# Two-stage DFT and mixture of experts on one core: the pass over the expert weights starts with the first batch, through four buffers

## The chip, the cores and the metric

One Trainium2 chip, one of its cores. The metric is device microseconds of the whole program, from the run's own time; a profile of one execution shows what each engine did. TensorE (PE) multiplies matrices, VectorE (DVE), ScalarE (ACT) and GpSimd (POOL) work on vectors, and SyncE (SP) issues most of the DMAs. Each engine works through its own list of instructions in order and waits at the head of that list.

## The reference, cut to what matters

```python
# x: 8 batches x 2496 rows x 256 columns
X = np.fft.fft(np.fft.fft(x, axis=1), axis=2).real
x = X.reshape(19968, 256)
e_idx = np.argmax(x @ w_gate, axis=1)            # one of 8 experts for each row
gate_w = softmax(x @ w_gate)[e_idx];  eom = sigmoid(x @ w_output_gate)
for e in range(8):
    mask = e_idx == e
    h = np.maximum(x[mask] @ w1[e], 0.0)         # w1[e]: 256 x 1024
    out[mask] = gate_w * eom * (h @ w2[e])       # w2[e]: 1024 x 256
```

## The kernel before

**Front end.** Each batch of `x` comes in five chunks `xt` of 512 KB. A chunk is folded in two parts: `fold1` (three instructions, most of them on POOL) and `fold2` (mostly DVE, result `ft`). The first DFT stage (`dstage`, matrices `tdet` and `tdot`) multiplies the five folded chunks, `devac` writes the result as a high and a low half in f16 (`ahi` on ACT, `alo` on DVE), and the second stage (`sstage`, tables `tst`, `tstm`, `tstr`, `tstq`) runs in five steps a batch. `sevac` turns a step's result into rows of the transform, `gating` picks the expert of each row, and 20 indirect DMAs a batch (`scatter`, tile `scr`), issued by POOL, write the rows into a scratch tensor sorted by expert. `steps` counts the steps over all batches: step n is step n % 5 of batch n // 5. Before a batch can be multiplied, its energy must be known: ACT squares the folded chunks (`sq`), DVE adds (`es`), PE sums over partitions, and `scale` makes a power of two from it.

**Weight energies.** The expert weights are split into f16 halves with a power of two for each expert and each matrix. For it every weight (16 tiles of 128x2048 f32, 1 MB each, `wt`) is loaded once, squared and summed on ACT (`wsquare`), and `wscales` makes the scales from the sums. The tiles have two buffers (`NW`); load k + 2 is issued by SP after square k.

**Expert stage.** The loop breaks out after step FSTART = 13, and from there the expert slots (256 rows of one expert at a time) are written down, with the rest of the front end paced between them. A slot fetches its rows (`xr`, a DMA transpose from `scr`; the first slots need the rows of batches 0 and 1), and its weights, raw (`raw0b`, `raw1b`), are converted to halves (`w0b`, `w1b`, L1093 on ACT and L1094 on DVE). `mm1` multiplies into `hp`, ACT and DVE write the halves `hh` and `hl`, `mm2` multiplies into `yp`, and ACT and POOL write the result out.

**Order.** While the front end runs, SP and POOL keep the order in which the code issues; the other engines' lists are put in order by a scheduler when the program is built. All loads of SP share one queue, and a load issued by SP waits at the head of SP's list until its buffer is free.

## Time and profile before

| | us |
|---|---|
| median of three runs | 1179.53 |
| the three runs | 1179.14, 1179.53, 1185.99 |
| the profiled execution | 1188.88 |
| its span | 1187.1 |
| PE busy in the span | 1064.3 (90%) |
| DVE, ACT, POOL busy | 835.8, 730.6, 517.4 |

The profiled execution took 9.35 us more than the median of the three timed runs; its span is 1.78 us shorter than its own time. Times in the rows are microseconds from the start of the span.

### The profile page before, as it was taken

The page shows a single profiled execution, that of the slowest core. Times are in us where ns is not written, and L with a number is a line of the kernel's source. Part 1 is how long each engine was busy: PE and PEld are TensorE (multiplying, and loading weights), DVE is VectorE, ACT ScalarE, POOL GpSimd, SP SyncE. Part 2 cuts the span into 40 slices and gives each one's busy share as a digit, 9 for nine tenths or more (in the row PEclk, how much of TensorE's full clock was granted, in tenths as well). Part 3 has the DMA queues.
Part 4 walks back from the last instruction along what each step waited for, and adds up shares of the span by engine and source line. Part 5 has one row for each costly group of instructions (what it writes and reads, how often), then busy time and mean ns, then how long its engine had stood idle before and what let it go on. Part 6 is the DMA issues. An engine that isn't in the chain of part 4 may idle for free.

```text
span 1187.1 us, 28726 instructions
## 1 busy us (share of the span) xinstructions
PE 1064.3 (90%) x10120; PEld 948.6 (80%) x10120; DVE 835.8 (70%) x1543; ACT 730.6 (62%) x1214; POOL 517.4 (44%) x450
## 2 busy tenths in 40 slices
PE   3686569989799998978999999999989999999998
PEld 3586559878698877767788888889879979998877
DVE  7996498786897747447544455487768767877785
ACT  2498667656576545444445445477767767777684
POOL 6728746866767643352475122222222222232232
PEclk8788779989999999989999999999999999999999
DMA  5688936655457554535676623576477764767641
GB/s 208 245 301 296 339 98 183 181 162 156 151 140 183 149 145 117 134 113 144 174 178 173 166 73 85 157 185 157 122 169 190 137 164 121 183 155 161 167 134 36
DMA packets 158213, 193.79 MB, mean 163 GB/s; under 512 B 117885, under 2 KB 118655, under 8 KB 156020
## 3 DMA queue, kind: packets, MB, share of 16 engines
q1 hardware_dynamic: 142100, 149.39, 47.7%
q0 software_dynamic: 15824, 42.14, 10.7%
q8 instruction: 79, 1.29, 0.5%
q10 hardware_dynamic: 144, 0.44, 0.2%
q14 instruction: 66, 0.54, 0.1%
HBM read 193.17 MB, written 43.46 MB: 199 GB/s over the span
## 4 chain that ended last, share of the span: by engine, by line
PE 61%; issue 9%; DVE 9%; ACT 6%; DMA 6%; POOL 5%; SPq 3%; another core or an unknown queue 1%; POOLq 0%; ACTq 0%; DVEq 0%
PE hp L1113 29%; PE yp L1133 28%; PE psb_t L504 3%; POOL scr L636 3%; DMA wt<-in_w_dram 2%; POOL out_dram L1141 1%; SPq L1055 1%; DMA raw1b<-in_w_dram 1%; ACT wt L356 1%; DVE w1b L1094 1%; ACT w1b L1093 1%; POOL xt L402 1%; DVE w0b L1094 1%; DVE hl L1118 1%
## 5 line engine op out<-in xcount | busy, mean ns | idle before, releaser
L1113 PE MATMUL hp<-xr,w0b 128*128 128x256 f16 (+2 forms) x4224 | 489.5, 265 | 28.7 <-DVE hl L1118 13.8
L1141 POOL DMA_INDIRECT out_dram<-y,xf x163 | 217.2, 1333 | 573.1 <-ACT y L1140 535.9
L1133 PE MATMUL yp<-w1b,hh 128*128 128x256 f16 x2608 | 451.9, 274 | 6.8 <-issue 5.9
L1113 PEld LDWEIGHTS <-w0b 128*128 128x128 f16 x4224 | 386.7, 99 | 85.1 <-issue 34.1
L1133 PE MATMUL yp<-w1b,hl 128*128 128x256 f16 (+3 forms) x1304 | 357.3, 274 | 3.1 <-issue 3.1
L1133 PEld LDWEIGHTS <-hh 128*128 128x128 f16 x2608 | 252.5, 99 | 40.9 <-issue 11.9
L1117 ACT ACTIVATE hh<-hp 128x512 f16<-128x512 f32 (+4 forms) x352 | 194.3, 555 | 129.7 <-PE hp L1113 108.9
L1118 DVE SCALAR_TENSOR_TENSOR hl<-hp,hh 128x512 f16<-128x512 f32 (+4 forms) x352 | 221.6, 635 | 73.8 <-ACT hh L1117 67.3
L1094 DVE SCALAR_TENSOR_TENSOR w1b<-raw1b,ssc,w1b 128x1024 f16<-128x1024 f32 x144 | 185.3, 1287 | 116.1 <-ACT w1b L1093 95.9
L1094 DVE SCALAR_TENSOR_TENSOR w0b<-raw0b,ssc,w0b 128x1024 f16<-128x1024 f32 x144 | 186.0, 1294 | 64.9 <-ACT w0b L1093 46.8
L1093 ACT ACTIVATE w0b<-raw0b,ssc 128x1024 f16<-128x1024 f32 x144 | 164.4, 1146 | 76.4 <-PE hp L1113 33.0
L636 POOL DMA_INDIRECT scr<-rows,desti x160 | 177.7, 1111 | 65.1 <-issue 43.3
L1093 ACT ACTIVATE w1b<-raw1b,ssc 128x1024 f16<-128x1024 f32 x144 | 165.1, 1148 | 60.3 <-PE yp L1133 25.2
L1133 PEld LDWEIGHTS <-hl 128*128 128x128 f16 (+3 forms) x1304 | 128.3, 98 | 19.7 <-issue 4.3
L1140 ACT ACTIVATE y<-yp,ysc 128x256 f32<-128x256 f32 (+1 forms) x163 | 69.0, 471 | 43.0 <-PE yp L1133 37.6
L467 PE MATMUL psb_t<-tdet,ft 128*125 128x145 f32 (+1 forms) x160 | 39.8, 334 | 26.8 <-DVE ft L428 10.2
L402 POOL TENSOR_TENSOR xt<-xt 128x500 f32<-128x500 f32 (+1 forms) x35 | 46.1, 1316 | 22.0 <-DMA xt<-in_xl_dram 12.2
L504 PE MATMUL psb_t<-ahi,tstq 125*128 125x145 f16 (+1 forms) x384 | 45.0, 237 | 7.9 <-DVE alo L478 5.8
L467 PEld LDWEIGHTS psb_t<-tdet,ft 128*125 128x125 f32 (+1 forms) x160 | 28.7, 219 | 28.3 <-issue 15.3
L504 PEld LDWEIGHTS <-tstq 125*128 125x128 f16 (+1 forms) x576 | 42.1, 103 | 9.2 <-issue 8.4
L477 ACT ACTIVATE ahi<-psb_t,p_x 125x580 f16<-125x580 f32 (+1 forms) x40 | 28.7, 740 | 29.0 <-DVE p_x L266 14.5
L504 PEld LDWEIGHTS <-tst 125*128 125x128 f16 (+1 forms) x384 | 30.9, 108 | 16.9 <-issue 13.7
(210 smaller groups left out, 953.5 us busy)
## 6 DMA issues: line engine op xcount, KB each, us to landing
raw0b<-in_w_dram SPq DMA_DIRECT2D x144, 512.0 KB
raw1b<-in_w_dram SPq DMA_DIRECT2D x144, 512.0 KB
xt<-in_xl_dram SPq DMA_DIRECT2D x40, 512.0 KB
wt<-in_w_dram SPq DMA_DIRECT2D x16, 1024.0 KB
out_dram<-y,xf POOLq DMA_INDIRECT x163
scr<-rows,desti POOLq DMA_INDIRECT x160
xr<-scr SPq DMA_TRANSPOSE x88
xf<-scr SPq DMA_DIRECT2D x75, 2.0 KB
```

The costliest lines, as they stand in the source:

```text
L402: eng.tensor_tensor(x0, x0, x1, op=ALU.add)
L467: nc.tensor.matmul(o[:, 0:145], ft[:, 0, par, W], tdet, start=True, stop=False)
L504: nc.tensor.matmul(ps[:, k, c0:c0 + 145], tab[hl][t][K], a[K, kc, par, c0:c0 + 145], start=(n == 0), stop=(n == len(terms) - 1))
L636: free_order("scr", batch=b, inst=nc.gpsimd.indirect_dma_start(out=scr[:, :], out_offset=bass.IndirectOffsetOnAxis(ap=desti[:, j:j + 1], a ...
L1093: nc.scalar.activation(w[:, 0], r, AF.Copy, scale=sc)
L1094: nc.vector.scalar_tensor_tensor(w[:, 1], r, sc, w[:, 0], op0=ALU.mult, op1=ALU.subtract)
L1113: nc.tensor.matmul(ps[:, k, T], w1v[:, hl, kc, (f % 4) * 128:(f % 4 + 1) * 128], a["x"][:, x, T], start=(m == 0), stop=(m == 5))
L1117: nc.scalar.activation(hh[:, G, T], ps[:, :, T], AF.Relu)
L1118: nc.vector.scalar_tensor_tensor(hl[:, G, T], ps[:, :, T], 0.0, hh[:, G, T], op0=ALU.max, op1=ALU.subtract)
L1133: nc.tensor.matmul(a["yp"][0:M, u], a[k, h][:, f, u * 128:u * 128 + M], w2v[:, hl, f], start=(g == 0 and f == 0 and m == 0), stop=(h == 1 ...
L1140: nc.scalar.activation(a["y"][0:M, u], a["yp"][0:M, u], AF.Copy, scale=ys[0:M, u:u + 1])
L1141: free_order("out", nc.gpsimd.indirect_dma_start(out=out[:, :], out_offset=bass.IndirectOffsetOnAxis(ap=a["f"].bitcast(I32)[0:M, u, 1:2], ...
```

## The change

The first four weight loads are issued behind the first seven chunks of `x` and the two tables of steps 0 and 1. Four buffers rotate instead of two: the two `wt` tiles, and the two tiles of the raw weights of the first expert slots, which are now one tile of 128x2048 each with two halves as views. In `start`, one square follows each of the last four folds, and each square is followed by the load of the tile four places on; in `steps`, each step takes two squares, so that the sixteenth comes in step 5 and `wscales` in step 6, where they were spread over steps 2 to 12. FSTART stays at 13.

```diff
-W0, NW = 2, 2
+NW, WFIRST, WRATE = 2, 4, 2
...
         def wload(k):
             if k < 2 * E:
-                wq[k] = pw.tile([128, 2048], F32, name="wt", tag="wt", bufs=NW)
+                wq[k] = rawt[0][k % 2] if k // 2 % 2 == 0 else pw.tile([128, 2048], F32, name="wt", tag="wt", bufs=NW)
                 nc.sync.dma_start(wq[k], wsrc[k % 2][k // 2])
...
+        def wsquares(n):
+
+            for _ in range(n):
+                if wdone[0] < 2 * E:
+                    wsquare(wdone[0])
+                    wload(wdone[0] + 2 * NW)
+                elif wdone[0] == 2 * E:
+                    wscales()
+                wdone[0] += 1
+
+        wdone = [0]
...
         def start():
             gt_ = gate_tables()
             next(gt_)
+            for j in range(2):
+                load_t(j)
+            for k in range(2 * NW):
+                wload(k)
             for c in range(KC):
                 fold1(0, c, nc.gpsimd if c % 2 else nc.vector)
...
                 weave(fold2(0, c))
+                if c >= KC - WFIRST:
+                    wsquares(1)
                 if c > 2:
                     dstage(0, c - 3)
-            for j in range(2):
-                load_t(j)
             nc.sync.dma_start(tidt, tid)
...
-                while wk <= 2 * E and wk < (n - W0 + 1) * (2 * E + 1) / (FSTART - W0):
-                    if wk < 2 * E:
-                        wsquare(wk)
-                        wload(wk + NW)
-                    else:
-                        wscales()
-                    wk += 1
-                if n == W0 - 1:
-                    for k in range(NW):
-                        wload(k)
+                wsquares(WRATE)
                 yield ("step", n)
...
-        raw, wbuf = [], []
+        rawt, raw, wbuf = [], [], []
...
-            raw.append([[p_.tile([128, 1024], F32, name=f"raw{m}b{i}{h}", bufs=1) for h in range(2)] for m in range(2)])
+            rawt.append([p_.tile([128, 2048], F32, name=f"raw{m}b{i}", bufs=1) for m in range(2)])
+            raw.append([[rawt[i][m][:, h * 1024:h * 1024 + 1024] for h in range(2)] for m in range(2)])
```

Three places show what moved. The first is SP's list at the start of the program, before the change, from the loads of the first chunks (seven at once, five more as folds free their buffers) to the first two weights:

```order
L297 DMA xt<-in_xl_dram 128x1024 x11
L916 DMA tst_111<-in_ts_dram 128x2048 x2
L931 DMA tidt<-in_tid_dram 128x160
L933 DMA scr<-ztile 128x258 x2
L916 DMA tstm<-in_tsm_dram 128x2560
L916 DMA tstr<-in_tsr_dram 128x1536
L916 DMA tstq<-in_tsq_dram 128x2048 x2
L297 DMA xt<-in_xl_dram 128x1024 x5
L352 DMA wt<-in_w_dram 128x2048 x2
```

And with the change (weights go to `raw0b`, `raw1b` and `wt` in turn):

```order
L352 DMA raw0b_141<-in_w_dram 128x2048
L352 DMA raw1b_142<-in_w_dram 128x2048
L352 DMA wt<-in_w_dram 128x2048 x2
L297 DMA xt<-in_xl_dram 128x1024 x2
L352 DMA raw0b_141<-in_w_dram 128x2048
L352 DMA raw1b_142<-in_w_dram 128x2048
L297 DMA xt<-in_xl_dram 128x1024 x2
L352 DMA wt<-in_w_dram 128x2048
L297 DMA xt<-in_xl_dram 128x1024
L352 DMA wt<-in_w_dram 128x2048
L947 DMA tidt<-in_tid_dram 128x160
L949 DMA scr<-ztile 128x258 x2
```

Eight weight loads stand ahead of `tidt` and the tables `tstm`, `tstr` and `tstq`, and chunks 7 to 11 (the eighth to the twelfth load of `xt`) stand between them.

The second place is PE's list around the energy sum of batch 1 (`psm_t<-es`). Before, it stands behind the 60 matmuls of step 2 (tables `tstm`, `tstr`), and the first stage of batch 1 follows:

```order
L504 LDWEIGHTS tstr
L504 MATMUL psb_t<-alo,tstr 128x145
L504 LDWEIGHTS tstr
L504 MATMUL psb_t<-ahi,tstr 128x145
L447 MATMUL psm_t<-es,cs 128x1
L467 MATMUL psb_t<-tdet,ft 125x145
```

With the change it stands ahead of them:

```order
L480 MATMUL psb_t<-tdot,ft 125x80
L481 MATMUL psb_t<-tdot,ft 125x145
L459 MATMUL psm_t<-es,cs 128x1
L516 LDWEIGHTS tstm
L516 MATMUL psb_t<-ahi,tstm 128x145
L516 LDWEIGHTS tstm
L516 MATMUL psb_t<-alo,tstm 128x145
```

So step 2 of batch 0 now waits for the energy of batch 1.

The third place is DVE's list ahead of the first `hl` of the expert stage. Before, from the last fold of chunk 24 (64 columns a half) on, with the gating of batch 2 (`r_mx` and what follows) on both sides of it:

```order
L428 TENSOR_TENSOR ft<-xt 128x2x64
L430 TENSOR_TENSOR ft<-xt 128x2x64
L1137 TENSOR_SCALAR ysc<-xf,ssc_76 128x2
L570 TENSOR_TENSOR r_mx<-r_mx,cs 128x20
L1118 SCALAR_TENSOR_TENSOR hl<-hp,hh 128x512
L535 TENSOR_TENSOR rows<-rt,rows 128x4x129
L573 TENSOR_TENSOR r_oh<-cs,r_mx 128x160
```

With the change:

```order
L428 TENSOR_TENSOR ft<-xt 128x2x128
L615 TENSOR_TENSOR r_t<-r_t,r_oh 128x160
L431 TENSOR_TENSOR xt<-xt 128x2x128
L618 TENSOR_REDUCE r_dest<-r_t 128x20
L440 TENSOR_TENSOR ft<-xt 128x2x64
L442 TENSOR_TENSOR ft<-xt 128x2x64
L1142 TENSOR_SCALAR ysc<-xf,ssc_76 128x2
L621 TENSOR_TENSOR desti<-r_dest,cs 128x20
L1123 SCALAR_TENSOR_TENSOR hl<-hp,hh 128x512
L455 TENSOR_REDUCE es<-en 128x1
```

The last fold of chunk 24 still stands ahead of `hl`; the gating of batch 2 is all ahead of it.

## Rows read from the trace of the kernel before

**Rows 1.** Busy time by stretch of the span, 200 us and later: length, then PE, weight loads (PEld), DVE, ACT and POOL busy with their counts, granted clock of PE as a share of full speed, busy share of the DMA engines, GB/s.

```profile
200.00:240.00 40.00, 36.89 (x378) 33.54 (x376) 32.62 (x61) 28.76 (x57) 33.81 (x30) 1.00 0.61 189
700.00:800.00 100.00, 100.00 (x919) 89.63 (x917) 58.86 (x74) 58.41 (x85) 25.67 (x20) 1.00 0.48 130
```

**Rows 2.** The same view of the first 180 us, the same columns.

```profile
0.00:30.00 30.00, 11.50 (x52) 10.89 (x52) 21.56 (x42) 8.49 (x16) 18.28 (x24) 0.90 0.57 210
30.00:60.00 30.00, 18.92 (x163) 18.23 (x164) 28.50 (x46) 13.08 (x36) 22.88 (x24) 0.73 0.67 247
60.00:90.00 30.00, 26.00 (x265) 25.26 (x265) 26.55 (x79) 28.03 (x56) 8.33 (x9) 0.86 0.81 302
90.00:120.00 30.00, 20.51 (x205) 19.12 (x204) 20.34 (x66) 24.68 (x51) 24.45 (x24) 0.83 0.87 291
120.00:150.00 30.00, 15.36 (x134) 14.36 (x132) 14.99 (x58) 19.49 (x32) 22.40 (x23) 0.77 0.87 327
150.00:180.00 30.00, 20.56 (x153) 18.28 (x153) 29.24 (x68) 18.08 (x40) 12.75 (x13) 0.77 0.35 97
```

**Rows 3.** The chain of work that ended last, in order of time: start, length, what. The loads of weights in it, and the landing of the last scatter of batch 1.

```profile
90.06 7.76 DMA wt<-in_w_dram
...
116.93 6.31 DMA wt<-in_w_dram
...
126.71 8.33 DMA wt<-in_w_dram
...
153.28 2.97 DMA scr<-rows,desti
```

**Rows 4.** POOL in order of time: start, length, line, operation, and in brackets the idle time ahead of it with what ended it. First and last scatter of batch 0, first and last of batch 1, and the end of the fold of chunk 24.

```profile
86.94 1.14 POOL L636 DMA_INDIRECT scr<-rows,desti  x1 [15.20 <-DVE rows L630]
...
118.25 1.26 POOL L636 DMA_INDIRECT scr<-rows,desti  x1 [0.30 <-issue]
122.86 0.97 POOL L636 DMA_INDIRECT scr<-rows,desti  x1 [3.35 <-ACT rows L539]
...
153.28 1.05 POOL L636 DMA_INDIRECT scr<-rows,desti  x1 [0.30 <-issue]
...
163.01 0.90 POOL L404 TENSOR_TENSOR xt<-xt 128x256 f32<-128x256 f32 x1
```

**Rows 5.** PE and DVE in order of time at the first expert slot: the first expert matmuls, the last DVE instruction on chunk 24, and the first `hl`.

```profile
167.88 4.07 PE L1113 MATMUL hp<-xr,w0b 128*128 128x256 f16 x24
...
171.59 0.28 DVE L430 TENSOR_TENSOR ft<-xt 128x128 f32<-128x128 f32 x1
...
172.02 0.68 DVE L1118 SCALAR_TENSOR_TENSOR hl<-hp,hh 128x512 f16<-128x512 f32 x1
```

**Rows 6.** The instructions on the tile `wt`: the squares, with the shortest, median and longest time in ns, first and last start in us.

```profile
L356 ACT ACTIVATE wt<-wt x16: 1895/1910/1923, 66.7 to 139.5; 128x2048 f32<-128x2048 f32 x16
```

**Rows 7.** Busy time by stretches of 3 us, the columns of rows 1: DMA share and GB/s stand last, the granted clock ahead of them.

```profile
12.00:15.00 3.00, 0.00 (x0) 0.00 (x0) 2.93 (x7) 2.14 (x4) 2.58 (x3) 1.00 0.79 313
15.00:18.00 3.00, 1.48 (x6) 1.48 (x7) 2.97 (x4) 0.00 (x0) 2.84 (x4) 1.00 0.00 0
...
30.00:33.00 3.00, 2.47 (x11) 2.50 (x12) 3.00 (x5) 0.71 (x2) 2.92 (x5) 0.50 1.01 365
...
42.00:45.00 3.00, 3.00 (x31) 3.00 (x29) 2.12 (x6) 2.00 (x7) 0.00 (x0) 0.63 1.04 412
...
51.00:54.00 3.00, 0.55 (x9) 0.36 (x6) 3.00 (x4) 0.00 (x0) 2.92 (x4) 1.00 0.00 0
54.00:57.00 3.00, 0.00 (x0) 0.00 (x0) 3.00 (x5) 1.39 (x3) 2.92 (x4) 0.57 0.00 0
57.00:60.00 3.00, 1.81 (x7) 1.76 (x8) 2.85 (x11) 2.97 (x11) 1.41 (x2) 0.50 0.72 249
```

**Rows 8.** PE in order of time around the energy sum of batch 1: first matmul of step 2, the last, the energy sum, the first of step 3.

```profile
47.56 0.23 PE L504 MATMUL psb_t<-ahi,tstm 125*128 125x145 f16 x1
...
51.32 0.23 PE L504 MATMUL psb_t<-ahi,tstr 128*128 128x145 f16 x1
57.95 0.59 PE L447 MATMUL psm_t<-es,cs 128*128 128x1 f32 x2 [6.40 <-DVE es L443]
...
64.45 0.33 PE L504 MATMUL psb_t<-ahi,tstq 125*128 125x145 f16 x1
```

**Rows 9.** ACT in order of time, from the end of the energy of batch 1 to the last ACT instruction that the scatter of batch 0 waits for (`r_ez`): one square of a chunk, the cast and a tile of `tidt`, the first `ahi` of batch 1, two copies of rows, `r_ez`.

```profile
57.73 0.63 ACT L438 ACTIVATE sq<-ft 128x500 bf16<-128x500 f32 x1
...
59.10 0.61 ACT L534 CAST rows<-rt 128x516 f16<-128x516 f32 x1
59.62 0.19 ACT L632 COPY rows<-tidt 128x4 int32<-128x4 int32 x1
59.71 1.37 ACT L477 ACTIVATE ahi<-psb_t,p_x 125x580 f16<-125x580 f32 x2
...
62.57 0.61 ACT L538 COPY rows<-rows 128x508 f16<-128x508 f16 x1
...
84.92 0.30 ACT L593 ACTIVATE r_ez<-r_za,lsc 128x20 f32<-128x20 f32 x1
```

**Rows 10.** POOL's wait for chunk 12, and two DVE instructions on chunks beside it and one without a POOL fold beside it.

```profile
45.54 1.25 POOL L402 TENSOR_TENSOR xt<-xt 128x500 f32<-128x500 f32 x1 [4.90 <-DMA xt<-in_xl_dram]
...
48.98 2.31 DVE L416 TENSOR_TENSOR ft<-xt 128x250 f32<-128x250 f32 x2
...
71.82 0.40 DVE L416 TENSOR_TENSOR ft<-xt 128x250 f32<-128x250 f32 x1
```

## What the prediction was, before any run of the changed kernel

> **What bounds the kernel now.** I read the stretches of the span first. From 700 us on PE is busy in every microsecond, and already from 200 us on in 36.89 of 40 [rows 1]. What ends that part is the matmul work of the expert slots, so a change ahead of it counts by as much as it moves the start of the slots, and by no more. The first 180 us are another matter: no engine is full there, and the DMA share is 0.57 in the first 30 us, 0.67 in the next, 0.87 from 90 to 150 [rows 2].
>
> Second, the chain of waits: it goes three times through the load of a weight tile, 7.76, 6.31 and 8.33 us, together 22.4 us [rows 3]. Taken alone that row promises some 22 us.
>
> Third, POOL in order of time, which says something else. The first slots need the rows of batches 0 and 1, 40 scatters in POOL's list, and these run almost end to end: batch 0 from 86.94 to 119.51, a gap of 3.35, batch 1 from 122.86 to 154.33 [rows 4]. Chunks of later batches are folded between them, in the same order before and after. The landing then takes until 156.25 [rows 3], and `xr` follows. So the weight loads that the chain names hold up the front end's steps, but of the scatters only those 3.35 us. What starts POOL's row is the gating of batch 0, for which POOL waited 15.20 us [rows 4]; and there ACT is full, 28.03 of 30 us [rows 2].
>
> Fourth, the first `hl` of the slots: it comes at 172.02, 8.1 us after the fold of chunk 24 ended on POOL at 163.91 [rows 4, 5]. DVE works off the gating of batch 2 and late steps in between, 29.24 of 30 us busy [rows 2]. That backlog is the second thing that late weight loads cost.
>
> **The change part by part.** The profiled execution took 1188.88 us, 9.35 above the median; the sum is made against it and the difference put on the median.
>
> *Removed: the waits of steps 7 to 12 for weights.* The last square is in step 5 instead of 12; front-end steps up to the break then run at the engines' pace and are through while POOL still scatters. Worth (a) the 3.35 us gap [rows 4], since batch 1's gating is ready before POOL has done batch 0; (b) the backlog. In the new list the last DVE instructions on chunk 24 still stand ahead of the first `hl`, with two of the gating and `ysc`; at 0.3 to 0.4 us for a fold instruction [rows 5, 10] some 2.2 us from the end of POOL's fold instead of 8.1, so 5.9 us. The first expert matmuls, 4.07 us long [rows 5], fit ahead of it: the rows land some 6 us after POOL's last scatter, the fold ends 9.6 us after it (154.33 to 163.91). Together 9.3 us, if the first scatter stays where it is. The cover of (a) is POOL's own queue: were the gating of batch 1 over 3 us late again, (a) is gone.
>
> *Added: sixteen squares earlier.* Each takes 1.91 us and some 0.1 for its sum [rows 6]. Ahead of `r_ez` of batch 0 there were five; now there are thirteen. Eight of these, 16 us, fall before 60 us, where ACT has 16.9 us free in 30 us [rows 2]; from the first `ahi` of batch 1 on it is five as before. I cost the eight at nothing as long as their tiles have landed.
>
> *Moved: the loads.* The DMA queue is empty from 15 to 18 us and from 51 to 57 [rows 7], so it has room. At about 370 GB/s (365 and 412 when it is full [rows 7]) what stands ahead of chunk 12, and it, are two tables (1.0 MB), eight weights (8.4), five chunks (2.6), `tidt`, the scratch rows and four tables (2.4), and 0.5: 15.0 MB from 15 us on, 41 us, and with a pause or two where SP waits for a square, 57 us instead of 45.54 [rows 10]. SP's list is in order, and weight k + 4 waits for square k, so chunks 9 to 16 and the tables wait behind squares. On the same count chunk 14 comes at 65 and chunk 17 at 75. POOL then still folds chunk 17 before 80 us, ahead of the first scatter; batch 1 needs only chunks 5 to 9, and chunk 9 comes at about 42. So its energy is ready at about 57 us, as before (57.95 [rows 8]).
>
> *Moved: step 2 of batch 0.* This is the cost that I find. PE's list now has the energy sum of batch 1 ahead of the 60 matmuls of step 2, which took from 47.56 to 51.55 [rows 8]. They wait until about 57.5 us, after an idle stretch; the granted clock after such a stretch was 0.50, from 57 to 60 us [rows 7], that is 1.2 of 2.4 GHz, so they take 4.0 us at the full clock and up to 8 at half; I take 7, and the first stage behind them then runs at the full clock, which gives 3 back. Step 3 starts some 3 to 4 us late against 64.45 [rows 8]. On ACT the evacuation of step 2 falls behind the first `ahi` of batch 1: ACT's list from there to `r_ez` is nine entries longer, at the start-to-start times of the rows [rows 9] a square of a chunk 0.75, two casts 1.0, two copies of rows 1.0, two of `tidt` 0.2, two from PSUM 0.5, in all 3.4 us; and ACT first waits some 2 to 3 us for step 2. Full as ACT is, the two add: 5.5 us on `r_ez` (84.92 [rows 9]) and on the first scatter. Bounds: below, 0, if ACT finds other work in the wait and DVE runs faster where POOL waits for chunks; above, 15, if loads come late as well (third rival). I take 5.5, nearest to the rows.
>
> *The sum:* 3.35 + 5.9 - 5.5 = 3.8 us gained, 1185.1 for the profiled execution and 1175.7 for the median. From there the slots carry it to the end, since PE sets their pace [rows 1]. The new form of the raw tiles, one with two views, moves no load of the slots: their waits stay per half. I cost it at nothing.
>
> **The rivals.** *First: the first scatter does not move.* ACT's free time takes in step 2 as well. For it speaks that ACT has so much room before 60 us; against it, that step 2 now hangs on the energy. Gain 9.3, time 1170.
>
> *Second: the folds that move collide.* Two DVE instructions on a chunk took 2.31 us beside POOL's folds, one without a fold beside it 0.40 [rows 10], so a pair is 1.5 us longer. In 30 to 60 us POOL was busy 22.88 us, in 60 to 90 only 8.33 [rows 2]; three or four folds, 9 to 12 us, now move into the second stretch, where DVE has 3.5 us left. At 1.5 us a fold at most DVE loses 5 us there and becomes the bound: the first scatter is 10 us late, the gain is gone, 1180. Against it: there DVE reads mostly PSUM or other tiles. The Trainium skill, page "SBUF — State Buffer", section "SBUF: two separate sides", says that GpSimd and a DVE operation with two SBUF inputs hold one port pair in turn, each for its whole instruction. The two rows agree; by that rule alone every fold that moves would delay DVE by its full length, and the time would be this rival's.
>
> *Third, the slower side: SP's list holds up the chunks.* Chunks 14 to 16 stand behind the loads of weights 8 and 9, and these behind squares 4 and 5, in the middle of ACT's work for steps 1 and 2. If these squares slip by 8 us (a tile late, or `ahi` ahead of them), chunk 14 lands at 73 instead of 65; its `fold2` stands in DVE's list ahead of the gating of batch 0, so everything behind it waits, PE's next steps too. The first scatter is then 5.5 + 8 = 13.5 us or more late; from 9.3 on the change is slower. Time: 1179.5 - 9.3 + 13.5 to 15 = 1184 to 1185, more if the loop closes twice. For it speaks POOL's wait of 4.90 us for chunk 12 [rows 10], with tables and no weight ahead of it.
>
> **How the numbers follow.** The forecast has 0.48, with 1172 to 1178 as its own range; the first rival 0.20, the second 0.16, the third 0.16. Predicted is 1175.7. To leave out no more than 0.2 the range takes in the first rival and most of the third: 1167 to 1187, where the lower end is the first rival less the spread of the rows. A measurement of this kernel can tell a change of about 1%, 11.8 us. Faster by over that needs the first rival and 2 us more from the expert stage: 0.14. Slower by over 1% needs a first scatter 21 us late: 0.05. Within 1%: 0.81.
>
> **What would show it.** Right: no wait of ACT for a weight after 90 us; the DMA full from 15 to 85 us; batch 0's first scatter between 90 and 95 us; no gap between the 20th and 21st scatter; the first `hl` some 76 us after the first scatter. The first rival is right if the first scatter stays at 87; the second if DVE has no idle time from 60 to 90 and the scatter is at 97; the third if DVE or POOL waits for a chunk after 65 us. I am wrong altogether if the first `hl` moves and the end does not, or if the scatters of batch 1 wait for their gating again.

## The result, and the profile after

The changed kernel took 1188.4 us (median of 20 runs, 1180.4 to 1193.9), the kernel before 1180.4 us in as many runs beside it (1172.0 to 1187.7). The ratio is 1.0069 with an interval of 1.0049 to 1.0090: slower by 0.7%, where 0.3% faster was forecast. The profiled execution of after took 1188.94 us with a span of 1187.2, close to its median; that of before (1188.88) was 8 us above its own, so the two spans are no comparison of the kernels. The ratios, here and below, leave out executions in the slow state; there was one, of e13, at 6070 us.

The lines of after carry other numbers: what is L402 to L636 in [rows 1 to 10] stands 12 lines lower, what is over L1000 five lines lower (`hl` is L1123, the scatter L648). First the stretches of 30 us, the columns of [rows 2], of the kernel after:

```profile
0.00:30.00 30.00, 12.77 (x59) 12.52 (x60) 21.21 (x46) 9.89 (x17) 14.44 (x20) 0.89 0.94 367
30.00:60.00 30.00, 15.73 (x135) 15.23 (x134) 21.36 (x40) 26.05 (x47) 16.09 (x19) 0.73 0.93 361
60.00:90.00 30.00, 23.23 (x253) 22.16 (x251) 26.21 (x65) 23.25 (x49) 15.42 (x16) 0.87 0.80 315
90.00:120.00 30.00, 20.72 (x205) 19.90 (x203) 20.00 (x65) 22.84 (x49) 21.42 (x21) 0.87 0.41 150
120.00:150.00 30.00, 19.26 (x162) 17.05 (x160) 15.77 (x66) 9.27 (x21) 23.96 (x25) 0.78 0.53 176
150.00:180.00 30.00, 13.29 (x93) 12.22 (x94) 27.49 (x65) 16.55 (x35) 19.27 (x17) 0.61 0.24 74
```

The transfers moved as meant: DMA share 0.94 and 0.93 in the first two stretches against 0.57 and 0.67, and 0.41 where it was 0.87. In the third row DVE is as busy as before, 26.21 us, with 65 instructions instead of 79, and POOL, 8.33 us there before, has 15.42.

POOL of the kernel after in order of time, the row that answers to [rows 4]: first scatter, last of batch 0 and first of batch 1, the last three, and the end of the fold of chunk 24.

```profile
94.45 1.15 POOL L648 DMA_INDIRECT scr<-rows,desti  x1 [16.45 <-ACT qs L532]
...
126.36 0.97 POOL L648 DMA_INDIRECT scr<-rows,desti  x1 [0.31 <-issue]
127.64 0.97 POOL L648 DMA_INDIRECT scr<-rows,desti  x1 [0.30 <-issue]
...
155.41 1.29 POOL L648 DMA_INDIRECT scr<-rows,desti  x1 [0.30 <-issue]
157.01 1.73 POOL L648 DMA_INDIRECT scr<-rows,desti  x1 [0.31 <-issue]
159.04 2.56 POOL L648 DMA_INDIRECT scr<-rows,desti  x1 [0.30 <-issue]
...
170.08 0.90 POOL L416 TENSOR_TENSOR xt<-xt 128x256 f32<-128x256 f32 x1
```

The first scatter is 7.5 us late. The gap of 3.35 us between the batches is gone, and yet the 40 scatters take 67.15 us from first to last, as long as with the gap (67.39): the last three need 1.29, 1.73 and 2.56 us, where those of before took 1.05, 1.06 and 1.05, and the own times of all 40 add up to 44.25 us instead of 41.64. The fold of chunk 24 ends at 170.98, 7.1 us late.

The start of the expert slots in the kernel after, which answers to [rows 5], PE first and then DVE:

```profile
178.54 5.28 PE L1118 MATMUL hp<-xr,w0b 128*128 128x256 f16 x24 [3.51 <-DMA xr<-scr]
...
180.65 0.28 DVE L442 TENSOR_TENSOR ft<-xt 128x128 f32<-128x128 f32 x1
...
182.00 0.68 DVE L1123 SCALAR_TENSOR_TENSOR hl<-hp,hh 128x512 f16<-128x512 f32 x1
```

The first `hl` is 9.98 us late: 7.51 by the first scatter, less 0.24 and 0.20 in scatters and folds, and 2.91 between the last fold and `hl`, which is 11.0 us instead of 8.1. Those 2.9 us have a row of their own: PE now waits for `xr`. SP's queue in the kernel after (start, length from first to last issue, count):

```profile
137.05 34.22 SPq L297 DMA_DIRECT2D xt<-in_xl_dram  x3
172.80 1.72 SPq L1092 DMA_DIRECT2D raw0b<-in_w_dram  x2
175.27 1.34 SPq L1078 DMA_TRANSPOSE xr<-scr  x1
```

The third chunk load waits 33 us for an `ft` on DVE, and `xr` stands behind it, asked for 13.7 us after the last scatter's end; before it was 1.9 us (156.27). The front end of batch 2 had stood still for a while, which is part of why DVE was that late, not all of it: in e5 below the same row of SP is 27.39 us long without such a standstill. PE in the kernel after, step 1 of batch 2, with the idle time ahead of an instruction in brackets:

```profile
128.90 0.34 PE L480 MATMUL psb_t<-tdot,ft 128*125 128x80 f32 x2
129.69 0.28 PE L481 MATMUL psb_t<-tdot,ft 128*125 128x145 f32 x1 [0.46 <-issue]
130.42 0.28 PE L481 MATMUL psb_t<-tdot,ft 128*125 128x145 f32 x1 [0.44 <-issue]
131.15 0.38 PE L479 MATMUL psb_t<-tdet,ft 128*125 128x145 f32 x1 [0.44 <-issue]
```

From 129 to 136 us PE starts one matmul or weight load every 0.72 us, waiting for nothing that the profile shows. It does so again from 146 to 151 us.

### The profile page after: what moved, and what is told of

It reads as the page before. It is cut to its first block, busy times and chain, and to the rows that moved or that the text cites. A ratio compares the mean times of both kernels' runs of the same rounds, so it can differ in the third digit from the quotient of the medians.

```text
span 1187.2 us, 28733 instructions
## 1 busy us (share of the span) xinstructions
PE 1063.2 (90%) x10120; PEld 949.4 (80%) x10120; DVE 832.7 (70%) x1543; ACT 732.9 (62%) x1214; POOL 518.7 (44%) x450
## 3 DMA queue, kind: packets, MB, share of 16 engines
q8 instruction: 79, 1.29, 0.5%
## 4 chain that ended last, share of the span: by engine, by line
PE 61%; issue 12%; DVE 11%; POOL 6%; DMA 4%; ACT 3%; SPq 1%; another core or an unknown queue 1%; POOLq 0%; DVEq 0%; ACTq 0%
PE hp L1118 29%; PE yp L1138 28%; PE psb_t L516 3%; DMA xt<-in_xl_dram 2%; POOL scr L648 2%; POOL out_dram L1146 2%; POOL xt L414 1%; DVE w1b L1099 1%; DVE rt L544 1%; DVE rows L547 1%; DVE hl L1123 1%; DMA raw1b<-in_w_dram 1%; DVE ft L428 1%; DVE w0b L1099 1%
## 5 line engine op out<-in xcount | busy, mean ns | idle before, releaser
L1123 DVE SCALAR_TENSOR_TENSOR hl<-hp,hh 128x512 f16<-128x512 f32 (+4 forms) x352 | 221.4, 636 | 72.8 <-ACT hh L1122 67.6
L648 POOL DMA_INDIRECT scr<-rows,desti x160 | 180.2, 1126 | 63.4 <-issue 44.0
L1098 ACT ACTIVATE w0b<-raw0b,ssc 128x1024 f16<-128x1024 f32 x144 | 164.5, 1146 | 67.6 <-PE hp L1118 39.9
L1098 ACT ACTIVATE w1b<-raw1b,ssc 128x1024 f16<-128x1024 f32 x144 | 165.2, 1148 | 58.4 <-PE yp L1138 31.7
L516 PE MATMUL psb_t<-ahi,tstq 125*128 125x145 f16 (+1 forms) x384 | 48.5, 244 | 7.8 <-DVE alo L490 4.5
L490 DVE SCALAR_TENSOR_TENSOR alo<-psb_t,p_x,ahi 125x580 f16<-125x580 f32 (+1 forms) x40 | 32.2, 814 | 20.7 <-ACT ahi L489 18.6
```

The lines of the kernel that those rows point to most:

```text
L516: nc.tensor.matmul(ps[:, k, c0:c0 + 145], tab[hl][t][K], a[K, kc, par, c0:c0 + 145], start=(n == 0), stop=(n == len(terms) - 1))
L648: free_order("scr", batch=b, inst=nc.gpsimd.indirect_dma_start(out=scr[:, :], out_offset=bass.IndirectOffsetOnAxis(ap=desti[:, j:j + 1], a ...
L1098: nc.scalar.activation(w[:, 0], r, AF.Copy, scale=sc)
L1123: nc.vector.scalar_tensor_tensor(hl[:, G, T], ps[:, :, T], 0.0, hh[:, G, T], op0=ALU.max, op1=ALU.subtract)
```

## The experiments

Each set of runs has its own runs of the kernel before beside it, and every ratio is against those; their level moved between the sets (1143 us in all but the last, 1187 us in that one), so times of different levels are not compared. The table has what the profile of each run shows, in us: first scatter, the time from its start to the end of the 40th, the idle time between the 20th and 21st, the time from the end of the 40th to the end of POOL's fold of chunk 24, the time from there to the first `hl`, and that `hl`. A dash stands where that fold is no longer behind the scatters. Each row is one profiled execution; the ratios of e9 and e10 rest on six executions of the changed kernel, those of the others on nine to twenty.

| kernel | ratio to before, interval | first scatter | 40 scatters | gap | folds | to `hl` | first `hl` |
|---|---|---|---|---|---|---|---|
| before, [rows 4, 5] | 1 | 86.94 | 67.39 | 3.35 | 9.58 | 8.11 | 172.02 |
| after | 1.0069 (1.0049 to 1.0090) | 94.45 | 67.15 | 0.31 | 9.38 | 11.02 | 182.00 |
| e1 before, raw tiles as one | 0.9997 (0.9977 to 1.0017) | 86.37 | 64.85 | 0.31 | 9.59 | 8.10 | 168.91 |
| e2 after, no energies | 0.9996 (0.9970 to 1.0023) | 88.64 | 67.62 | 0.30 | 8.33 | 5.54 | 170.13 |
| e3 after, squares from step 4 | 1.0011 (0.9992 to 1.0030) | 86.75 | 71.63 | 3.65 | 8.94 | 6.74 | 174.06 |
| e4 after, chunk load behind `xr` | 1.0035 (1.0013 to 1.0056) | 94.47 | 68.48 | 0.31 | 8.52 | 3.21 | 174.68 |
| e5 after again | 1.0024 (1.0011 to 1.0038) | 94.42 | 68.72 | 0.31 | 8.50 | 3.88 | 175.52 |
| e6 after, no square in the start | 1.0039 (1.0026 to 1.0053) | 89.69 | 72.24 | 6.73 | 8.94 | 6.96 | 177.83 |
| e7 after, one square a step | 1.0041 (1.0025 to 1.0057) | 92.98 | 69.14 | 0.31 | 9.05 | 4.71 | 175.88 |
| e8 after, no DVE half of slot 0 | 1.0013 (1.0000 to 1.0026) | 93.92 | 65.57 | 0.31 | 8.33 | 5.58 | 173.40 |
| e9 after, three folds on DVE | 1.0065 (1.0048 to 1.0082) | 94.29 | 70.87 | 2.74 | - | - | 176.30 |
| e10 before, three folds on DVE | 0.9946 (0.9930 to 0.9962) | 87.24 | 66.15 | 0.41 | - | - | 166.62 |
| e11 before, five folds on DVE | 0.9968 (0.9944 to 0.9992) | 87.77 | 69.93 | 0.72 | - | - | 167.07 |
| e12 after, short squares | 1.0017 (0.9998 to 1.0036) | 94.97 | 66.65 | 0.30 | 8.36 | 4.22 | 174.20 |
| e13 e3 and three folds on DVE | 1.0019 (1.0003 to 1.0034) | 86.83 | 76.07 | 6.84 | - | - | 171.54 |
| e14 e2 and three folds on DVE | 0.9976 (0.9959 to 0.9993) | 87.39 | 69.35 | 0.31 | - | - | 165.82 |
| e15 after, four loads later | 1.0054 (1.0022 to 1.0087) | 90.77 | 69.38 | 3.39 | 9.19 | 6.48 | 175.82 |

**e1: the raw tiles alone.** In the kernel before:

```diff
-raw.append([[p_.tile([128, 1024], ..., bufs=1) for h in range(2)] for m in range(2)])
+rawt.append([p_.tile([128, 2048], ..., bufs=1) for m in range(2)])
+raw.append([[rawt[i][m][:, h * 1024:h * 1024 + 1024] for h in range(2)] for m in range(2)])
```

> The kernel before, with only one part of the change: the first set of raw weights (and the later one) is two tiles of 128x2048 with views of halves instead of four tiles of 128x1024. Loads and squares of the energies stay as before. Theory LATE FRONT END (the whole loss is the first scatter of POOL, 94.45 us after against 86.94 us before, and its followers): time of before within 0.3%, 1180 us, first scatter at about 87 us. Rival SHARED TILE (a load of one half now waits for the readers of the other half, 288 loads of raw weights long): the loss of about 8 us shows here, 1186 to 1190 us. Rival ORDER (the conversions of slot 0 stand ahead of the second folds of chunk 22 on DVE, and so hold SP's list): no loss here, since the weight energies stay late.

No loss (0.9997): sharing the tiles costs nothing. The run is at the same time a second look at the schedule of before, and there POOL has no gap between the batches. POOL of e1, the 20th and 21st scatter and the last:

```profile
119.26 0.97 POOL L636 DMA_INDIRECT scr<-rows,desti  x1 [0.30 <-ACT wt L356]
120.53 1.19 POOL L636 DMA_INDIRECT scr<-rows,desti  x1 [0.30 <-ACT qb L519]
...
150.17 1.05 POOL L636 DMA_INDIRECT scr<-rows,desti  x1 [0.30 <-issue]
```

**e2: no energies at all.**

```diff
-wq[k] = rawt[0][k % 2] if k // 2 % 2 == 0 else pw.tile(...)
-nc.sync.dma_start(wq[k], wsrc[k % 2][k // 2])
+wq[k] = None
...
-nc.scalar.activation(wt, wt, AF.Square, accum_out=wen[:, k:k + 1])
+if k == 0:
+    nc.vector.memset(wen, 4.0)
```

> The kernel after without the loads and squares of the weight energies: a constant stands in the place of the sixteen energies, so the scales of the weights are not worked out from them. All else of the change stays. LATE FRONT END, by the transfers or the squares: the first scatter comes back to 87 us or earlier, and the time to 1180 us or lower; what lies under the 1180 us of before is what the energies still cost there (the three waits for a weight and the gap between the 20th and 21st scatter, together 3 to 9 us: 1171 to 1177 us). ORDER: the fold of chunk 22 stays behind the conversions on DVE, xr stays over 8 us behind the last scatter, and the time stays within 3 us of the kernel after, 1185 to 1189 us. SHARED TILE: 1186 to 1189 us.

0.9996 of before. With 16.8 MB of loads and 16 squares gone, the kernel is no faster than with them late. So leaving the weights out gains nothing on balance. Its first `hl` is 1.2 us later than that of e1: the folds and the time to `hl` are 3.8 us shorter, but the first scatter comes 2.3 us later and the 40 scatters take 2.8 us longer. What the waits in the chain of before [rows 3] cost apart from that is not shown. Against the kernel after, the first scatter comes back to 88.6; the 40 scatters still take 67.6 us.

**e3: loads early, squares from step 4.**

```diff
-NW, WFIRST, WRATE = 2, 4, 2
+NW, WFIRST, WRATE = 2, 0, 2
...
-wsquares(WRATE)
+if n > 3:
+    wsquares(WRATE)
```

> The kernel after with its loads as early as there (four buffers filled behind the first x chunks), but no square before the step after the first scatter: two a step from step 4 on. LATE FRONT END by squares and by PE's order (step 2 of batch 0 behind the energy sum of batch 1): first scatter back at 87 to 89 us, time 1180 to 1183 us. LATE FRONT END by transfers (8 MB of weights ahead of the chunks of batch 1 and 2): here only 4 MB stand ahead, the first scatter is at 89 to 92 us, time 1182 to 1185 us. ORDER: the conversions still stand ahead of the folds of chunk 22 on DVE, so 1185 to 1188 us.

The first scatter is back at 86.75, with half of the loads ahead of the chunks and no square ahead of step 4. The time is 1.0011, not to be told from before: 6.8 us more between the first and the last scatter than in e1 (a gap of 3.65 and slower scatters) take the rest.

**e4: SP's chunk load behind `xr`.** The third load that `fold2` asks for from step 11 on is issued behind the first two `xr`:

```diff
-load_x()
+if hold[0] is None or hold[0] < 2:
+    load_x()
+if hold[0] is not None:
+    hold[0] += 1
...
 chained(load_x_, 1)
+hold[0] = None
+load_x()
```

> The kernel after with one transfer moved on SP: the third chunk load behind the first raw weights, the one that waited until 171.3 us for DVE, is issued behind the first two xr instead of ahead of them. Nothing else moves. ORDER: xr is asked for at once after the last scatter (about 163 us instead of 175.3), the first matmul of the experts starts 3 to 10 us earlier than 178.5 us and the time falls by 3 to 8 us, 1180 to 1185 us. LATE FRONT END: xr is asked for earlier too, but the first hl still stands behind the folds on DVE: the time is within 1.5 us of the kernel after, 1187 to 1190 us. SHARED TILE: no change, 1188 us.

**e5: the kernel after again.**

> The kernel after, unchanged, on the chip of the other experiments (the kernel before takes 1143 us there). It is the measure for the others: the kernel with the chunk load behind xr came out 0.35% over the kernel before there. ORDER: the kernel after stands 3 to 8 us over that one, at 1151 to 1155 us, xr 8 us or more behind the last scatter. LATE FRONT END: within 1.5 us of it, at 1146 to 1149 us.

e4 stands at 1.0035, e5, without its edit, at 1.0024, with intervals that overlap: moving the chunk load gains nothing here, because in e5 the list does not hold `xr` up in the first place. SP's queue in e5:

```profile
132.34 27.39 SPq L297 DMA_DIRECT2D xt<-in_xl_dram  x3
161.28 1.73 SPq L1092 DMA_DIRECT2D raw0b<-in_w_dram  x2
165.32 1.34 SPq L1078 DMA_TRANSPOSE xr<-scr  x1
```

The chunk load still waits for DVE, but `xr` comes 2.2 us after the last scatter (163.14), not 13.7. PE issues no matmul at intervals of 0.72 us in the profile of e5. The 2.9 us at `hl` that the profile of after lost there are not lost in this one; what is left of the change in e5 is 0.24%, 0.11 to 0.38%. Its POOL (first scatter, three beside the conversions of slot 0, last fold of chunk 24), and the conversions on DVE:

```profile
94.42 1.14 POOL L648 DMA_INDIRECT scr<-rows,desti  x1 [17.39 <-ACT qs L532]
...
144.02 1.27 POOL L648 DMA_INDIRECT scr<-rows,desti  x1 [0.30 <-issue]
145.59 1.73 POOL L648 DMA_INDIRECT scr<-rows,desti  x1 [0.30 <-issue]
147.62 2.56 POOL L648 DMA_INDIRECT scr<-rows,desti  x1 [0.30 <-issue]
...
170.74 0.90 POOL L416 TENSOR_TENSOR xt<-xt 128x256 f32<-128x256 f32 x1
```

```profile
143.15 1.28 DVE L1099 SCALAR_TENSOR_TENSOR w0b<-raw0b,ssc,w0b 128x1024 f16<-128x1024 f32 x1
...
145.18 1.28 DVE L1099 SCALAR_TENSOR_TENSOR w0b<-raw0b,ssc,w0b 128x1024 f16<-128x1024 f32 x1
146.38 2.48 DVE L1099 SCALAR_TENSOR_TENSOR w1b<-raw1b,ssc,w1b 128x1024 f16<-128x1024 f32 x2
```

**e6 and e7: fewer squares ahead of the first scatter.** In e6 none among the folds of batch 0 (`WFIRST` 0, so that weights 4 to 7 are asked for behind chunks 9 to 12 too); in e7 one a step instead of two (`WRATE` 1).

> The kernel after without the four squares that stand among the folds of batch 0: loads as early as there, two squares a step from step 0 on. If the four squares among the folds (7.6 us of ACT before 60 us) hold up the first scatter: 86 to 88 us, time 1143 to 1146 us. If two squares a step hold it up (LATE FRONT END by squares in the steps): 92 to 95 us, time 1146 to 1151 us.

> The kernel after with one square a step instead of two, the four squares among the folds of batch 0 kept. If two squares a step hold up the first scatter: 88 to 91 us (some four squares of 1.9 us fewer on ACT ahead of it), time 1143 to 1146 us. If the four among the folds or the early transfers do: 93 to 95 us, time 1146 to 1151 us.

The first scatter moved to 89.69 and to 92.98, in between what the expectations allow for, and neither time fell under that of e5. In e6 a gap of 6.73 us opened between the batches, 13 us after the last square (ACT, 106.1 to 108.0 us). So no square stands in the gap; but the chain of that profile runs over squares on ACT from 82 to 104 us, so it stays open whether early squares make the gating of batch 1 late.

**e8: no DVE half of slot 0's conversions.** The low halves of slot 0's weights are zeros, so that part of the first slot's product is left out.

```diff
-nc.vector.scalar_tensor_tensor(w[:, 1], r, sc, w[:, 0], ...)
+if n:
+    nc.vector.scalar_tensor_tensor(w[:, 1], r, sc, w[:, 0], ...)
```

> The kernel after without DVE's half of the four conversions of slot 0: the low halves of slot 0's weights are zeros set at the start, so the first slot's product lacks its low part. If these conversions slow the scatters beside them (1.29, 1.73 and 2.56 us instead of 0.98 in the trace of after): the 40 scatters take 41 to 42.5 us in sum instead of 44 to 45, the last one ends 3 us earlier, and the time is 3 to 5 us under the kernel after (part of it the 5 us that DVE has less to do). If not: scatters as in after, time within 2 us of the kernel after.

Without them the 40 scatters take 65.57 us instead of 68.72, and the sum of their own times is 42.4 us instead of 45.6. So the conversions cost the scatters 3.2 us. The three that take 1.27, 1.73 and 2.56 us in e5 are these in e8:

```profile
143.34 1.03 POOL L648 DMA_INDIRECT scr<-rows,desti  x1 [0.30 <-issue]
144.68 0.98 POOL L648 DMA_INDIRECT scr<-rows,desti  x1 [0.30 <-issue]
145.97 1.02 POOL L648 DMA_INDIRECT scr<-rows,desti  x1 [0.30 <-ACT qb L538]
```

In the time little of it is left: 1.0013 against 1.0024, with intervals that overlap.

**e9 to e11: POOL's folds behind the last scatter go to DVE.** In e9 (after) and e10 (before) chunks 22 to 24, in e11 (before) chunks 20 to 24:

```diff
-fold1(*divmod(m, KC), nc.vector if m % KC == 1 and m // KC < 3 else nc.gpsimd)
+fold1(*divmod(m, KC), nc.vector if m % KC == 1 and m // KC < 3 or 22 <= m <= 24 else nc.gpsimd)
```

> The kernel after with the first folds of chunks 22, 23 and 24 on DVE instead of POOL, where they stand behind the last of the 40 scatters (8.5 us of POOL, 163.1 to 171.6 us, in the kernel after on this chip; the first hl stands 3.9 us behind them). SERIAL POOL (the experts begin when POOL has done its scatters and these folds, and the weight energies were not on that chain): the first hl comes 4 to 7 us earlier than 175.5 us and the time falls by 2 to 5 us under the 1145.3 us of after, to 1140 to 1143 us. Rival DVE (the experts wait for the amount of work on DVE, which gets 4.9 us more): first hl within 2 us of 175.5 us, time 1144 to 1147 us.

> The kernel before with the same three folds on DVE. SERIAL POOL: first hl 2 to 6 us earlier than the 168.9 us of the kernel before with raw tiles as one, time 1138 to 1141 us against 1143.4 us. Here DVE still has the conversions and 8 us of backlog behind the folds, so the gain may be smaller than in the kernel after. Rival DVE: first hl at 169 to 172 us, time 1143 to 1146 us.

> The kernel before with the first folds of chunks 20 to 24 on DVE: two more folds (5.4 us of POOL) leave the chain between the scatters, so the last scatter ends at 145 to 147 us instead of 151.2 us. SERIAL POOL: time 1135 to 1140 us. Rival DVE: 8 us more work on DVE than before in the 65 us up to the first hl, first hl at 169 to 174 us, time 1143 to 1147 us.

In the kernel before this (e10) is a gain of 0.54% (0.38 to 0.70%), the largest of all versions here. The last scatter and the first `hl` of e10, POOL and then DVE:

```profile
152.33 1.06 POOL L636 DMA_INDIRECT scr<-rows,desti  x1 [0.30 <-issue]
...
166.62 0.68 DVE L1118 SCALAR_TENSOR_TENSOR hl<-hp,hh 128x512 f16<-128x512 f32 x1
```

That `hl` is 2.3 us ahead of the one of e1, while the time fell by some 6 us; the rest of the gain is not explained. In the kernel after the same edit (e9) loses: with its first scatter at 94.29, its last one ends at 165.16 and the transposes follow at 169.52, 4.4 us behind it instead of the 2.2 of e5, since a chunk load that waits for DVE stands ahead of them in SP's list again, so `hl` comes at 176.30 without any fold between. That is 0.8 us later than in e5, and the time went to 1.0065, worse than the `hl` says; the rest of that is not explained. Two more folds (e11) slow the scatters beside them (52.4 us in sum) and give part back.

**e12: short squares.** The energies then cover 128 of 2048 columns:

```diff
-nc.scalar.activation(wt, wt, AF.Square, ...)
+nc.scalar.activation(wt[:, 0:128], wt[:, 0:128], AF.Square, scale=4.0, ...)
```

> The kernel after with each square over 128 of the 2048 columns of its weight, so that ACT needs some 0.3 us for one instead of 1.9 us; the loads and their places stay, the energies cover a sixteenth of the weights. On PE, step 2 of batch 0 still stands behind the energy sum of batch 1. ACT TIME (the squares' own time in ACT's list delays the front end): first scatter at 86 to 89 us, time 1140 to 1144 us. PE ORDER (the waits for x of batch 1 ahead of step 2): first scatter at 91 to 94 us, time 1143 to 1147 us.

The first scatter stays at 94.97. So ACT's time on squares is not needed for the delay. On PE the 60 matmuls of step 2 end at 58.4 us in the chain of e12, against 62.5 in e5, and that did not help either: PE's order with that step behind the energy sum is not shown to be the cause by this run, though it stands so in it. Busy time from 45 to 75 us, the columns of [rows 2], of e12:

```profile
45.00:60.00 15.00, 7.56 (x78) 7.56 (x78) 10.11 (x27) 8.82 (x29) 4.72 (x6) 0.66 1.01 382
60.00:75.00 15.00, 11.36 (x149) 10.99 (x148) 14.60 (x19) 8.54 (x24) 12.95 (x14) 1.00 1.02 416
```

And of e3, whose first scatter came at 86.75:

```profile
45.00:60.00 15.00, 6.18 (x62) 5.94 (x60) 13.38 (x29) 7.78 (x22) 8.87 (x11) 0.76 0.45 162
60.00:75.00 15.00, 13.96 (x158) 13.56 (x158) 14.93 (x32) 9.77 (x21) 7.47 (x8) 0.90 0.56 212
```

In e12 the DMA is full to the end, POOL's folds fall into the second stretch (12.95 us against 7.47), and DVE does 19 instructions there in 14.60 us, 0.77 us each, where e3 has 32 in 14.93, 0.47 each. Single instructions show it; DVE of e12 beside POOL's folds, in order of time:

```profile
68.35 1.46 DVE L440 TENSOR_TENSOR ft<-xt 128x250 f32<-128x250 f32 x1
69.73 0.93 DVE L442 TENSOR_TENSOR ft<-xt 128x250 f32<-128x250 f32 x1
70.58 0.81 DVE L490 SCALAR_TENSOR_TENSOR alo<-psb_t,p_x,ahi 128x580 f16<-128x580 f32 x1
71.31 1.67 DVE L547 TENSOR_TENSOR rows<-rt,rows 128x516 f16<-128x516 f32 x1
```

With no fold beside them such instructions take 0.41, 0.41 and (the last, in e5) 0.69 us; `alo`, which reads PSUM, is the one that is not longer.

**e13 and e14: early energies, and none, with the three folds on DVE.** e3 and e2 with the edit of e10.

> The kernel with early loads and squares from step 4 on, and the first folds of chunks 22 to 24 on DVE, as in the fast version of the kernel before (1136.2 us, ratio 0.9946). SERIAL POOL: with a first scatter at 87 us and three folds off POOL's tail it comes out as that one does, 1135 to 1139 us; if the early energies are worth anything once POOL's tail is gone, 1131 to 1134 us. LATE SCATTERS (the conversions of slot 0 beside the last scatters and a gap ahead of batch 1's cost 5 us): 1139 to 1143 us.

> The kernel without loads and squares of the weight energies (a constant in their place), and the first folds of chunks 22 to 24 on DVE. It is the most that any earlier energies can give in the fast version. If the energies are worth nothing there either (SERIAL POOL): 1134 to 1138 us, like the fast version of before (1136.2 us). If the waits for a weight now end last there: 1128 to 1133 us.

Even with POOL's tail gone, a kernel without any energies (0.9976) is not faster than the one with late energies (0.9946). Early ones (1.0019) lose to both, with a gap of 6.84 us and slow scatters.

**e15: weights 4 to 7 asked for later.** The four squares among the folds of batch 0 stay; the next four move with their loads, from steps 0 and 1 to steps 2 and 3.

```diff
-wload(wdone[0] + 2 * NW)
+if wdone[0] >= WFIRST:
+    wload(wdone[0] + 2 * NW)
...
-wsquares(WRATE)
+if n == 1:
+    for k in range(2 * NW, 2 * NW + WFIRST):
+        wload(k)
+if n > 1:
+    wsquares(WRATE)
```

> The kernel after with the four loads that follow the squares of batch 0 (weights 4 to 7, 4.2 MB) asked for behind step 1 instead of ahead of chunks 9 to 12; the four squares among the folds of batch 0 stay, and two squares a step from step 2 on. TRANSFERS (weights ahead of the chunks push POOL's folds of chunks 12 to 17 to 58 to 78 us, where they and DVE's instructions slow each other, and the list of PE is made for these times): POOL folds 8 us or more between 45 and 60 us, DVE's instructions between 60 and 75 us take 0.45 us in the mean instead of 0.63 to 0.77, first scatter at 86 to 89 us, time 1141 to 1145 us. SQUARES (the four among the folds of batch 0): first scatter at 92 us or later, 1145 to 1149 us.

POOL and DVE did as TRANSFERS says: between 60 and 75 us POOL is busy 7.35 us and DVE does 30 instructions in 14.35 us, 0.48 each:

```profile
60.00:75.00 15.00, 13.67 (x157) 13.27 (x157) 14.35 (x30) 12.35 (x23) 7.35 (x9) 0.91 0.99 399
```

The first scatter came at 90.77, between the two expectations, and the time did not follow: 1.0054, in the set at 1187 us, so by this run an earlier first scatter gained nothing. Together with the others: the first four loads and no square ahead, 86.8 (e3); two squares a step without the four loads, 89.7 and 90.8 (e6, e15); the loads with hardly any squares' time, 95.0 (e12); both, 94.4 (e5). So the loads are enough for the whole delay, whatever the squares take. They also put step 2 behind the energy sum in PE's list, and both that order and the slow DVE come and go with them (in e3, e6 and e15 the order is the old one), so how much of it goes by the one and how much by the other stays open; that step 2 ended 4 us earlier in e12 for no gain speaks for DVE.

## Why the prediction was wrong

**The sum at the first `hl`.** The prediction had -3.35 (gap), -5.9 (backlog), +5.5 (first scatter): 3.8 us earlier. Between e1 and e5, two profiles without the stall on PE, the terms are: first scatter +8.05, the 40 scatters +3.87, folds -1.09, fold to `hl` -4.22; in sum 6.61 us later, which is 168.91 to 175.52. Set against the forecast: the scatters with their gap became 3.87 us longer instead of 3.35 shorter, the first scatter 8.05 later instead of 5.5, and the time from the fold to `hl` 4.22 shorter instead of 5.9. Nor does PE carry every microsecond of that on to the end, as the sum had it: the ratio of e5 is 0.24%, 2.7 us of 1143 (its median is 1.9 us above that of before), and e9 and e10 moved in time by more than their `hl` did. On the runs of the result itself it was 8 us.

**What bounds the kernel.** That the chain's 22 us for weights are mostly no cost was right: with all loads and squares gone no time is gained on balance (e2, and e14 with POOL's tail away). The first `hl` stands behind POOL's row from the first scatter to the fold of chunk 24, and e10, which takes folds off the end of that row at late energies, gains. The step that failed is what the sum made of that row: it booked the gap of 3.35 us as what late weights cost there, let the 40 scatters themselves keep their lengths, and priced the first scatter too low. Between e1 and e5 the gap was worth nothing, the scatters' own times grew by 3.8 us (41.8 to 45.6; 3.2 of it the conversions of slot 0, e8), and the first scatter came 8.05 us later. That is more than the backlog gave.

**(a) The gap.** It was taken from one execution. With the same schedule e1 has none (0.31 us), and with early energies it is 3.65, 6.73 and 6.84 us in e3, e6 and e13. It is the time by which batch 1's gating misses POOL. Late weights alone do not make it (e10 and e11 have 0.41 and 0.72), and with no weights there is none (0.30 and 0.31 in e2 and e14); what makes it in e3, e6 and e13 stays open. Against e1 its worth was 0.

**The term that was missing.** Once the scales come early, slot 0's conversions run back to back on DVE beside scatters: 1.73 and 2.56 us instead of 0.98. In the list of before an instruction of 0.25 us stands between them and the scatters take 1.05, as DVE and then POOL of before show:

```profile
150.68 0.25 DVE L698 TENSOR_TENSOR r_p<-r_g,wsc 128x96 f32<-128x96 f32 x1
150.84 1.28 DVE L1094 SCALAR_TENSOR_TENSOR w0b<-raw0b,ssc,w0b 128x1024 f16<-128x1024 f32 x1
152.04 0.24 DVE L700 TENSOR_REDUCE ssc<-r_p 128x12 f32<-128x96 f32 x1
...
150.56 1.05 POOL L636 DMA_INDIRECT scr<-rows,desti  x1 [0.30 <-issue]
151.92 1.06 POOL L636 DMA_INDIRECT scr<-rows,desti  x1 [0.31 <-issue]
```

e8 gives the size, 3.2 us. The Trainium skill, page "SBUF — State Buffer", section "SBUF: two separate sides", says that GpSimd cannot write the descriptors of a DMA that it issues while DVE runs an operation in a 2-port performance mode. Here too scatters were held up beside DVE (2.56 us against 1.02 in e8); that the conversions, which read two operands in SBUF, run in such a mode or that the ports are the reason is shown by no run. The prediction used that page for the folds alone.

**(b) The backlog.** Direction right, and most of the size: 8.1 became 3.9 in e5 and 3.2 in e4, where 2.2 was forecast. In the profiled execution of after it became 11.0, by the row of SP above: `xr` behind a chunk load that waits for DVE. The prediction asked of SP's list what it does to chunks, not what a chunk does to `xr`.

**The first scatter.** Forecast 90 to 95 us, 5.5 late; measured 94.45, 7.5 late. The number was near and its reasons were not. ACT's fuller list is not needed for it (e12), and step 2's end does not set it there. What the loads do was priced at nothing: they landed as forecast (chunk 12's fold starts at 57.96, chunk 14's at 65.53, chunk 17's at 74.78), and the prediction then said that POOL still gets its folds done ahead of the first scatter. It does; but the folds now run beside the front end's work on DVE, and step 2 stands behind the energy sum. Without both the first scatter came at 90.8 (e15), and which of them holds it up was not separated.

**The squares and the raw tiles at nothing.** Right for the tiles (e1). For the squares right as far as ACT's room before 60 us goes; two a step later, with the loads that follow them, cost the first scatter some 3 to 4 us against e3 (e6, e15), and on top of the early loads the squares' length cost nothing (e12).

**The rivals.** The second, folds that collide with DVE, comes nearest: it had 97 for the first scatter and 1180, with a chance of 0.16. The longer DVE instructions beside the folds are seen (e12), that they alone set the first scatter is not, and its sign, DVE without idle time from 60 to 90 us, was met in part only (26.21 of 30 us busy). What happens to the scatters it left out as well. The first fell at once. The third did not happen: POOL's last wait for a chunk ahead of the first scatter is 2.2 us at 65.5, and no loop closed. The signs named for "right" nearly all came true (no wait of ACT for a weight after 90 us, a DMA full to 75 us, a first scatter between 90 and 95, no gap), with the time on the other side: only the last, `hl` 76 us after the first scatter, would have told, and it is 87.6 (81.1 in e5, 82.5 in e1). The chance of 0.81 for within 1% held.

**What stays open.** Why the change cost 0.69% in the first comparison and 0.24% in e5. In the first, and in the set of e15, all kernels were 40 us slower, and PE shows stretches in which it issues an instruction per 0.72 us; in the sets at 1143 us it shows none. The kernel before of the first comparison has such stretches too, but in its first 200 us only a single instruction, at 120 us. Between 500 and 600 us, PE busy 87.68 us in the kernel after of the first comparison, and 99.67 in e5:

```profile
500.00:600.00 100.00, 87.68 (x769) 74.89 (x769) 59.34 (x164) 44.31 (x76) 40.82 (x40) 0.93 0.56 143
```

```profile
500.00:600.00 100.00, 99.67 (x918) 88.53 (x916) 67.44 (x172) 51.16 (x83) 60.33 (x56) 1.00 0.76 191
```

That such a stretch fell on the front end of batch 2 in the one profile of after is seen; that it falls there in most executions was not shown.

## What to carry to other kernels

A wait that the chain names costs only what its removal gives: leave the waiting work out altogether first (e2), and if the time stays, see what has come in its place, and look for the engine whose row is full from end to end, here POOL, and take work off that (e10). Loads that move ahead delay what stands behind them, and the delayed work runs beside something else than before; ask which engine it will meet there. A gap seen in one execution is no term of a sum until a second one shows it.

## What the runs showed of the hardware

A scatter of POOL took 0.98 us alone, 1.05 beside DVE conversions with a short reduction between them, and 1.73 to 2.56 beside conversions that follow each other at once. DVE instructions with both inputs in SBUF took 2.3 to 3.6 times as long beside POOL's folds (1.46 for 0.41, 1.67 for 0.69), one that reads PSUM (`alo`) 0.81 as ever. PE issued one instruction per 0.72 us for 7 us on end with nothing in the profile that it waited for, in one level of the runs and not in the other.
